# Gated linear attention and a multiplicative FFN: attention products by halves of a chunk's keys, with the masks shared between VectorE and ScalarE

## Chip, cores, metric

One core of a Trainium2 chip. The metric is device time in microseconds (us) from the first to the last instruction, median over several executions; lower is better.

TensorE is PE in the profile (PEld its weight loads), VectorE is DVE, ScalarE is ACT, GpSimd is POOL. L359 is line 359 of that kernel; each kernel has its own line numbers. A matmul in fp32 is two passes, so the counts (x16) of passes are twice the products.

## The reference, cut

```python
# attention: 4 batches, 8 heads, 768 positions, 48 wide
for t in range(S):
    state = alpha[:, :, t, :, None] * state + einsum('bhd,bhe->bhde', k[:, :, t], v[:, :, t])
    y[:, :, t] = einsum('bhd,bhde->bhe', q[:, :, t], state)
# then, on the 3072 x 384 result x (1024 inner):
a, b = x @ w1, x @ w2
out = (a * b @ w3) @ w_out
```

## The kernel before

The sequence is cut into 24 chunks of 128 positions (6 for each batch). In a chunk TensorE makes five groups of products: the old state times q ("state"), the scores k·q, the transposes of the next chunk's q and k, the masked scores times v ("values"), and the outer products for the new state. After the scores VectorE sets the upper triangle of the keys to zero (the mask), and ScalarE copies the transposes out of their banks.

```python
def transposed(n):                       # ... transposes of all heads into two banks tp
    for half in range(2):
        nc.scalar.copy(qkT[:, :, :, ds(DP * half, DP)], tp[half])

def scores(n):
    for j in range(NP):
        for i in range(2):
            r = ds(DP * i, D)
            nc.tensor.matmul(sc[i][:, j, :], qkT[r, 0, j, :], qkT[r, 1, j, :], start=True, stop=True)
    for i in range(2):
        nc.vector.tensor_tensor(ms[:, i].bitcast(I32), sc[i].bitcast(I32), keep_bc, op=ALU.bitwise_and)

def attend(n):
    for j, i, to in heads:
        nc.tensor.matmul(to, vc[:, 2 * j + i, :], ms[:, i, j, :], start=..., stop=...)
    # ... two ScalarE copies of the banks to x, stored to memory
```

The gates x·w1 and x·w2 are exact products of split numbers on the full array. They start as soon as three chunks of x are there, in pieces between the attention's groups; in every fourth chunk (10, 14, 18, 22 counted from 0) there are no pieces left.

```python
for n in range(N + 1):
    # ... loads
    if n: attend_state(n - 1)
    if n < N: scores(n)
    transposed(n + 1)
    if n - 2 in begin: split_x(g, 0)     # ... and new gates queued
    pieces = (0, 3, 3, 2)[(n - 6) % 4] if n > 5 else 0
    # ...
    if n: attend(n - 1)
    outer(n)
    run(pieces > 0)                      # one gate piece: nine passes of 384 columns
    # ... decayed q and k of n + 2, logs, decays; run(pieces > 1), run(pieces > 2)
```

## Time and profile before

| what | value |
|---|---|
| time, median of 3 | 497.57 us (495.11 to 498.14) |
| profiled execution | span 494.5 us, mean granted clock 0.990 |
| first gate product starts | 65.6 us |
| last values product starts | 196.7 us |
| TensorE idle before the first gate / from there to the last values product | 19.2 / 6.5 us |
| from the last values product to TensorE's last pass | 293.9 us, no hole in TensorE (the run ends 3.9 us later) |

The three places in this table cut the run into the *front*, the *middle* (the section in which attention and gates mix) and the *tail*. They come from the starts of single passes in the trace.

### The profile page before, as it was taken

To read this page: it belongs to the slowest core of one execution; us is meant where nothing else is said; L and a number is where in the kernel's file an instruction comes from. 1 tells how busy PE (TensorE), PEld (TensorE's weight loads), DVE (VectorE), ACT (ScalarE), POOL (GpSimd) and SP (SyncE) were. 2 spreads that over 40 slices of the span, in tenths; PEclk is the share of its full clock that TensorE was granted. 3 is DMA by queue.
4 is the path that set the end of the run, shared out by engine and by line. 5 is a ranking of instruction groups with operands and counts; after the bars stand their busy time and mean duration, and the time that the engine had idled before them with its cause. 6 is when DMAs were issued, how large, how long until landed. Compare 5 with 4: busy or idle time off the path is not lost.

```text
span 494.5 us, 9992 instructions
## 1 busy us (share of the span) xinstructions
PE 464.9 (94%) x3808; PEld 423.9 (86%) x3808; DVE 370.0 (75%) x614; ACT 247.8 (50%) x461; POOL 40.0 (8%) x86
## 2 busy tenths in 40 slices
PE   3969779999999999999999999999999999999996
PEld 2747559899898978999999988888888999999996
DVE  2668998998898566999999769686433786667771
ACT  3666758776666553655555444544222533333330
POOL 3123132212102200000000000000000000000000
PEclk9998999999999999999999999999999999999999
DMA  9999999999887933555464433320001875556511
GB/s 174 203 219 199 244 201 229 221 193 254 151 225 144 269 115 113 176 180 198 155 198 156 154 118 117 118 91 34 32 33 56 232 222 178 175 177 175 177 49 48
DMA packets 148032, 79.12 MB, mean 160 GB/s; under 512 B 92176, under 2 KB 141840, under 8 KB 147984
## 3 DMA queue, kind: packets, MB, share of 16 engines
q1 hardware_dynamic: 146704, 78.40, 61.0%
q0 software_dynamic: 1280, 0.08, 0.5%
q8 instruction: 30, 0.49, 0.4%
q14 instruction: 18, 0.15, 0.1%
HBM read 56.40 MB, written 22.06 MB: 159 GB/s over the span
## 4 chain that ended last, share of the span: by engine, by line
PE 78%; DVE 8%; DMA 7%; ACT 3%; issue 2%; SPq 1%; POOL 0%; DVEq 0%; POOLq 0%; ACTq 0%
PE bank L416 40%; PE bank L420 19%; PE bank L465 8%; PE bank L359 2%; PE bank L384 2%; PE bank L282 2%; DMA raw<-in_moe_w_out_dram 2%; PE bank L459 1%; DMA dec<-ends 1%; PE bank L319 1%; DVE ms L362 1%; DVE qk L297 1%; DMA ac<-in_alpha_dram 1%; DMA ends<-e 1%; PE bank L378 1%
## 5 line engine op out<-in xcount | busy, mean ns | idle before, releaser
L416 PE MATMUL bank<-x,w 128*128 128x384 f32 x768 | 160.1, 342 | 0.0
L416 PEld LDWEIGHTS bank<-x,w 128*128 128x128 f32 x768 | 134.2, 188 | 4.8 <-issue 1.9
L418 ACT ACTIVATE t<-bank 128x384 f32<-128x384 f32 x152 | 74.2, 491 | 116.2 <-PE bank L416 101.1
L421 DVE SCALAR_TENSOR_TENSOR r<-bank,t 128x384 f32<-128x384 f32 x128 | 69.1, 552 | 38.5 <-ACT t L418 33.5
L420 PE MATMUL bank<-x,w 128*128 128x384 f32 x384 | 87.9, 336 | 1.5 <-ACT qkT L321 1.2
L420 PEld LDWEIGHTS bank<-x,w 128*128 128x128 f32 x384 | 68.7, 189 | 2.1 <-ACT qkT L321 1.5
L416 PE MATMUL bank<-w3o,ab 128*128 128x384 f32 x384 | 70.4, 334 | 0.0
L416 PEld LDWEIGHTS bank<-w3o,ab 128*128 128x128 f32 x384 | 66.9, 188 | 0.0
L465 PE MATMUL bank<-wo,w3T 128*128 128x384 f32 x128 | 42.6, 486 | 0.0
L200 ACT ACTIVATE rest<-raw 128x512 f32<-128x512 uint32 (+1 forms) x36 | 23.4, 649 | 27.8 <-DMA raw<-in_moe_w_dram 20.9
L420 PE MATMUL bank<-w3o,ab 128*128 128x384 f32 x192 | 37.1, 334 | 0.0
L465 PEld LDWEIGHTS bank<-wo,w3T 128*128 128x128 f32 x128 | 24.2, 189 | 14.9
L484 DVE TENSOR_TENSOR ab<-abl,ab 128x1024 fp32r<-128x1024 f32 x24 | 29.4, 1223 | 9.1 <-ACT ab L483 9.1
L432 DVE TENSOR_TENSOR ab<-r 128x384 f32<-128x384 f32 x64 | 35.5, 554 | 0.9
L483 ACT ACTIVATE ab<-abl 128x1024 fp32r<-128x1024 f32 x24 | 25.5, 1061 | 18.8 <-PE bank L420 18.8
L359 PE MATMUL bank<-qkT 48*128 48x128 f32 x384 | 30.8, 297 | 3.6 <-DVE ms L362 1.8
L321 ACT COPY qkT<-bank 128x512 f32<-128x512 f32 x48 | 25.8, 590 | 16.0 <-PE bank L319 16.0
L420 PEld LDWEIGHTS bank<-w3o,ab 128*128 128x128 f32 x192 | 33.6, 188 | 0.0
L362 DVE TENSOR_TENSOR ms<-bank,keep 128x512 int32<-128x512 int32 x48 | 31.2, 682 | 2.4 <-PE bank L359 2.4
L359 PEld LDWEIGHTS bank<-qkT 48*128 48x128 f32 x384 | 25.9, 198 | 8.2 <-issue 4.2
L205 ACT ACTIVATE power<-power,rebias 128x512 uint32<-128x512 uint32 (+1 forms) x36 | 25.1, 699 | 15.2 <-DVE power L204 15.0
L297 DVE TENSOR_TENSOR qk<-kq,e 128x768 f32<-128x768 f32 x24 | 22.8, 952 | 10.6 <-ACT e L288 9.9
(66 smaller groups left out, 526.7 us busy)
## 6 DMA issues: line engine op xcount, KB each, us to landing
abd<-ab SPq DMA_DIRECT2D x64, 192.0 KB, 2.4
abl<-abd SPq DMA_DIRECT2D x24, 512.0 KB, 4.5
raw<-in_moe_w_dram SPq DMA_DIRECT2D x16, 512.0 KB, 3.8
xT<-xd SPq DMA_DIRECT2D x12, 576.0 KB, 4.3
raw<-in_moe_w_dram SPq DMA_DIRECT2D x24, 256.0 KB, 5.0
kq<-in_k_dram SPq DMA_DIRECT2D x24, 192.0 KB, 5.1
kq<-in_q_dram SPq DMA_DIRECT2D x24, 192.0 KB, 5.1
v<-in_v_dram SPq DMA_DIRECT2D x24, 192.0 KB, 4.6
```

The source lines that it names most:

```text
L297: nc.vector.tensor_mul(qks[n % 3][:, :, :, 0:D], st.pop(("kq", n)), st.pop(("e", n)).rearrange("p i (h d) -> p i h d", h=H))
L321: nc.scalar.copy(qkT[:, :, :, ds(DP * half, DP)], tp[half])
L359: nc.tensor.matmul(sc[i][:, j, :], qkT[r, 0, j, :], qkT[r, 1, j, :], start=True, stop=True)
L362: nc.vector.tensor_tensor(ms[:, i].bitcast(I32), sc[i].bitcast(I32), keep_bc, op=ALU.bitwise_and)
L416: nc.tensor.matmul(p1, w[part][i], x[part][i], start=(part == i == 0), stop=(part == 1 and i == n - 1))
L418: nc.scalar.activation(t, p1, AF.Copy, scale=(1.0 + 1.0 / P) * scale)
L420: nc.tensor.matmul(p2, w[2][i], x[2][i], start=(i == 0), stop=(i == n - 1))
L421: nc.vector.scalar_tensor_tensor(to, p2, -scale, t, op0=ALU.mult, op1=ALU.add)
L432: nc.vector.tensor_mul(ab, *r)
L465: nc.tensor.matmul(po, w3T[:, j, :], wo[:, j, :], start=(j == 0), stop=(j == KF - 1))
L483: nc.scalar.activation(t[:, 0], ab, AF.Copy, scale=1.0 - 2.0 ** -13)
L484: nc.vector.tensor_sub(t[:, 1], ab, t[:, 0].bitcast(FP32))
```

## The change

The intent: in a chunk of 128 positions the keys of the second half never see the queries of the first, so a quarter of scores and values is zero. Cut in halves of the keys, that quarter need not be computed, and only the two diagonal blocks of 64 columns need a mask; the rest is a plain copy, which idle ScalarE can make. Two row halves may not write one bank of the values at once (the rule of banks that the prediction cites), so the values' products now come in two turns. The second turn must not start until the first is surely out; the program ensures it by a dependency on the second copy of the next chunk's transposes, which TensorE makes after the first turn.

```diff
     def transposed(n):
         for half in range(2):
-            nc.scalar.copy(qkT[:, :, :, ds(DP * half, DP)], tp[half])
+            st["copied"] = nc.scalar.copy(qkT[:, :, :, ds(DP * half, DP)], tp[half])
     def scores(n):
         for j in range(NP):
-            for i in range(2):
-                r = ds(DP * i, D)
-                nc.tensor.matmul(sc[i][:, j, :], qkT[r, 0, j, :], qkT[r, 1, j, :], start=True, stop=True)
+            for s in range(2):
+                for i in range(2):
+                    r = ds(DP * i, D)
+                    nc.tensor.matmul(sc[i][hf(s), j, 0:C - DP * s], qkT[r, 0, j, hf(s)], qkT[r, 1, j, DP * s:],
+                                     start=True, stop=True)
         for i in range(2):
-            nc.vector.tensor_tensor(ms[:, i].bitcast(I32), sc[i].bitcast(I32), keep_bc, op=ALU.bitwise_and)
+            nc.vector.tensor_tensor(ms[:, i, :, 0:DP].bitcast(I32), sc[i][:, :, 0:DP].bitcast(I32), keep_bc,
+                                    op=ALU.bitwise_and)
+            nc.scalar.copy(ms[0:DP, i, :, DP:], sc[i][0:DP, :, DP:])
-    def attend(n):
-        for j, i, to in heads:
-            nc.tensor.matmul(to, vc[:, 2 * j + i, :], ms[:, i, j, :], ...)
+    def attend(n, turn):
+        for j in range(HP):
+            for b in range(2):
+                for s in range(2):
+                    jj, i = b * HP + j, turn ^ s
+                    product = tc.keep_in_program_order(nc.tensor.matmul(
+                        to[jj, i][:, DP * s:], vc[hf(s), 2 * jj + i, :], ms[hf(s), i, jj, 0:C - DP * s], ...))
+                    if turn and first:
+                        tc.add_manual_dep(product.ins, st["copied"].ins.name, ...)
 # the loop:
         if n: attend_state(n - 1)
+        if n: attend(n - 1, 0)
         if n < N: scores(n)
         # ...
-        if n: attend(n - 1)
         outer(n)
         run(pieces > 0)
+        if n: attend(n - 1, 1)
```

Cut away: the smaller mask constant, the fixed order of the transposes, and an extra small copy that stands in for "copied" in the last two chunks.

## The prediction

> **What bounds the kernel now.** I read the page first, then the busy time by stretches of 50 us, the chain that ended last, the waits of each engine by stretch, the timeline of TensorE through single chunks, and last the starts of single passes in the trace.
>
> From the page (busy us and share of the span, instructions) and the view of stretches (start and end, length, then busy us of PE, PEld, DVE, ACT, POOL, granted clock, DMA share, GB/s):
>
> ```profile
> PE 464.9 (94%) x3808; PEld 423.9 (86%) x3808; DVE 370.0 (75%) x614; ACT 247.8 (50%) x461; POOL 40.0 (8%) x86
> ...
> 0.00:50.00 50.00, 35.77 (x432) 27.34 (x432) 30.44 (x56) 28.24 (x55) 13.74 (x40) 0.93 1.09 199
> 50.00:100.00 50.00, 42.45 (x578) 36.36 (x579) 46.76 (x80) 35.41 (x70) 11.18 (x16) 0.97 0.99 224
> 100.00:150.00 50.00, 49.30 (x610) 44.88 (x609) 43.30 (x74) 32.83 (x69) 8.43 (x16) 1.00 0.92 206
> 150.00:200.00 50.00, 46.78 (x604) 42.26 (x604) 34.87 (x63) 26.93 (x59) 6.67 (x14) 1.00 0.59 154
> 200.00:250.00 50.00, 50.00 (x290) 50.00 (x290) 49.05 (x94) 28.18 (x52) 0.00 (x0) 1.00 0.58 186
> ```
>
> The attention chunks, which the change touches, fill the first 197 us. To about 65 us TensorE idles often and VectorE's conversions, masks and products are the chain. From the first gate product (65.6 us) TensorE is the bound. From 197 us to the end, nearly 300 us, it runs without a hole, and nothing there is changed. So what counts is TensorE's own time between 65 and 197 us, its holes there, and when the first gate starts.
>
> The groups concerned (busy us, mean ns of one, idle before):
>
> ```profile
> L359 PE MATMUL bank<-qkT 48*128 48x128 f32 x384 | 30.8, 297 | 3.6 <-DVE ms L362 1.8
> L362 DVE TENSOR_TENSOR ms<-bank,keep 128x512 int32<-128x512 int32 x48 | 31.2, 682 | 2.4 <-PE bank L359 2.4
> L321 ACT COPY qkT<-bank 128x512 f32<-128x512 f32 x48 | 25.8, 590 | 16.0 <-PE bank L319 16.0
> ```
>
> A typical chunk in TensorE's timeline (start us, length; state, scores, transposes, values, outer products, then a gate):
>
> ```profile
> 136.04 0.67 PE L378 MATMUL bank<-qkT,T 48*64 48x128 f32 x16
> 136.64 1.16 PE L359 MATMUL bank<-qkT 48*128 48x128 f32 x16
> 137.63 0.66 PE L319 MATMUL bank<-ident,qk 64*128 64x64 f32 x16
> 138.23 1.09 PE L384 MATMUL bank<-ms,v 128*64 128x128 f32 x16
> 139.15 0.62 PE L331 MATMUL bank<-v,qk 128*64 128x48 f32 x16
> 139.70 1.33 PE L416 MATMUL bank<-x,w 128*128 128x384 f32 x6
> ```
>
> The reader is to take the differences of starts, not the lengths: scores 0.99 us, values 0.92, state 0.60, all with sixteen passes (an fp32 product is two). The starts of single passes show why. Scores and values go in pairs on two half arrays, a pair every 112 and 109 ns. The state products, on quarter arrays, go four at a time, also every 109 ns. So a wave of passes with 128 moving columns takes 109 ns whether two or four share it.
>
> **What the Trainium skill says.** "TensorEngine Tiling (Array Packing)", Key Properties: "Changing tiling mode (not just tile) drains the TensorE". The trace agrees: where shape of array changes, the last pass of one group to the first of the next is about 90 ns longer than within a group, and the first wave is longer too. State to scores: 199 and 207 ns against waves of about 110, 0.18 us in all. Transposes to values 153 and 154 against 62 and 109, 0.14 us. Outer products to a gate 152 and 279 against 58 and 173, 0.20 us. Gate to state 268 and 140 against 173 and 109, 0.13 us. "TensorE: Matmul & The Clock Gate", in Part 3 (what overlaps and what doesn't), says matmuls start and end in program order; in this trace a pass never starts before its predecessor. The same page (engine queue depths) says that ScalarE and VectorE are strict first in, first out; the trace orders them so, and I build on it below. "PSUM — Partial Sum Buffer", on bank collisions: two engines may not use the same bank and quadrant at once, and different row tiles may not write one bank at once. The kernel before has no pair that shows it; the changed program obeys it, with ScalarE's copy of a score bank waiting for VectorE's mask of it, and the values' products split in two turns.
>
> **The change part by part.**
>
> Scores. Eight products on half arrays become sixteen on quarters, 128 and 64 columns alternating. The triangle saves a quarter of the columns, but a wave of four lasts as long as its 128-column members, since the next wave's first product needs the same quarter. 32 passes in waves of four are 8 waves x 109 = 0.87 us, as against 8 x 112 = 0.90. Values: 32 passes, 8 waves x 109 = 0.87 us, exactly as now. So TensorE gains 0.03 us a chunk, about 0.5 us over the 16 chunks after the first gate.
>
> Switches of the array's shape. Now a chunk is gate, quarters (state), rows (scores, transposes), columns (values, outer), gate. After: gate, quarters (state, first turn of values, scores), rows (transposes), columns (outer), gate, quarters (second turn), gate. I counted them in the two programs' order from the first gate to the last values' product: 74 now, 97 after. 13 second turns stand between two gates. Into gates +13 at 0.20 = +2.6 us; into scores -16 at 0.18 = -2.9; into transposes +15 at about 0.16 (my estimate between the cases above) = +2.4; into outer products +13 at 0.14 = +1.8; two fewer others, -0.3. Sum +3.6 us; with the 0.5 gained, TensorE's own work grows by 3.1 us.
>
> Masks. VectorE takes 682 ns for 512 columns, and other reads of a bank 552 for 384 and 351 for 192, about 0.15 us plus 1.04 ns a column. 256 columns are 0.42 us. 48 of them: 12.6 us of VectorE's 370 go. In the chain before the first gate, from 35 to 65 us, there are the masks of some five chunks, ten x 0.26 = 2.6 us. TensorE, ScalarE and a busy DMA share that stretch, so I count 1.5 us.
>
> ScalarE. 48 copies of 256 columns at 394 ns (the row of the copies to x) are 18.9 us more. It was busy 60 to 70% between 60 and 150 us, so it doesn't become the bound, but its order matters, next.
>
> New waits. The first product of the second turn waits for the second copy of the next chunk's transposes, which stands in ScalarE's order behind the two score copies, which wait for the masks. Counted from the end of the scores: mask lag L, two masks 0.75, a score copy 0.4, two transposed copies 1.1, together L + 2.25 us. TensorE comes there after transposes, outer products and one gate piece, at about +3.0. So it stands when L exceeds some 0.6 us. In the trace before L was, for chunks 8 to 23 (counted from 0), 0.0, 1.0, 2.3, 0.7, 1.4, 0.2, 2.3, 1.9, 0.0, 0.8, 2.1, 1.3, 0.0, 2.0, 3.0, 0.0. In the chunks with gates I let the lighter VectorE take 0.4 us from each: 12, 15, 19 and 21 stand by about 0.4, 0.9, 0.3 and 0.9, together 2.5 us. In the four chunks without gates (10, 14, 18, 22) TensorE has nothing to fill with: state, second turn, first turn and scores now wait for masks, two score copies and the transposed copies in a row. Now the next scores start at +3.2 us and the values take 0.9 later; after, the second turn can start at about +3.7 and the scores at +4.7: 0.6 us each, 2.4 in all.
>
> Sum: -1.5 + 3.1 + 2.5 + 2.4 = +6.5 us on 497.6, thus 504.
>
> **The rivals.** First: VectorE's relief carries through. It is busy 47 of 50 us between 50 and 100 us, and three of the largest holes of TensorE there are its own:
>
> ```profile
> PE bank L319 <- DVE qk L297: 2.3, 1, 2.3
> PE bank L282 <- ACT la L266: 1.7, 1, 1.7
> PE bank L359 <- DVE ms L362: 0.6, 1, 0.6
> ```
>
> All holes between the first gate and 197 us make 6.4 us. Had the change removed them all, with 2.6 from the front and no new wait, 9.0 less 3.1 would leave -6 us: 491.5. Against it: the mask is replaced by a longer chain over two engines, so the holes with "DVE ms" hardly go.
>
> Second: ScalarE's strict order makes the new waits worse than I count. A score copy that waits for a mask also holds up the copies that free a gate's bank, and then gate products stand. With L not lowered at all, L - 0.6 sums to 4.7 us over the gate chunks; if each of the 12 loses another 0.4 to such holes and the short ones 1.5 each, that is 15.5 us of waits in place of 4.9: 515.
>
> Third: issue. 64 passes now follow one another at 27 ns each, where only 16 did. If the sequencer can't feed them, say 35 ns, each chunk loses 0.5 us, 8 us over 16 chunks: 512. The state products' 27 ns speak against it, though their queue had been filled during a gate.
>
> **Range and chances.** The first rival in full gives 491, the second or third in full 512 to 515; halves of them bound my range at 496 and 513. A gain over 2% (under 487.6) has no source: 4%. A loss over 2% (above 507.5) needs a good half of the second or third rival: 26%. Within 2%: 70%.
>
> **What would show each step.** Single passes of scores and values in waves of four at 109 ns: then no gain in TensorE's own time. If the 64-column members let the next wave in early (waves near 80 ns), scores and values together gain 0.4 us a chunk and the prediction is 6 us too high. Second turns followed by a gate whose first pass comes after 200 ns and first wave takes 280: the switches. Mask near 0.42 us, score copy near 0.39. In the waits, second turn on the transposed copies near 5 us in all; far more means the second rival, near zero makes the time 499 or less. First gate at 63 to 65 us. After the last values' product, the same 297 us to the end; if that differs, my picture is wrong.

## More of the kernel before

The prediction shows the page's totals, stretches, groups and chain; one row of the page that it does not show matters later, the granted TensorE clock in 40 equal slices, in tenths of full speed:

```profile
PEclk9998999999999999999999999999999999999999
```

Here 9 is 90% or more. Only one slice near 40 us is lower.

## The result

| | before | after |
|---|---|---|
| median, range, 4 runs each | 496.34 us (494.94 to 498.14) | 525.31 us (521.33 to 526.06) |
| ratio | | 1.0571 (1.0510 to 1.0631) |
| profiled span, mean clock | 494.5 us, 0.990 | 519.6 us, 0.962 |
| first gate product | 65.6 us | 68.9 us |
| last values product | 196.7 us | 223.4 us |
| TensorE idle, front / middle | 19.2 / 6.5 us | 20.0 / 14.4 us |
| tail | 293.9 us | 292.3 us |

A ratio here and below is the mean time of one kernel's runs over that of the other's of the same rounds, with a 95% interval, so not quite the ratio of the medians. Executions over 1.5% slower than the fastest of the same kernel are left out of the means.

The change costs nearly 29 us, far outside the predicted range. The profiled pair differs by 25.1 us, and all of that lies before the last values product. The page after, its totals and clock row, and the stretches of 50 us (start and end, length, busy us of PE, PEld, DVE, ACT, POOL, clock, DMA share, GB/s):

```profile
PE 481.4 (93%) x4576; PEld 430.7 (83%) x4576; DVE 361.4 (70%) x615; ACT 264.4 (51%) x517; POOL 37.0 (7%) x86
...
PEclk9978899989899699899999999999999999999999
```

```profile
100.00:150.00 50.00, 46.86 (x729) 40.03 (x729) 33.19 (x61) 32.60 (x73) 7.77 (x16) 0.90 0.81 179
150.00:200.00 50.00, 43.16 (x649) 37.27 (x647) 28.41 (x54) 25.83 (x61) 6.38 (x13) 0.90 0.62 150
```

Two things differ from before. Between 100 and 200 us, the two stretches shown, TensorE is idle more (3.1 and 6.8 us of each 50, before 0.7 and 3.2). And the clock, which was 1.00 in those stretches, is 0.90. Note also that TensorE's busy time rose by 16.5 us although its predicted extra work was 3: an instruction at a lower clock is busy for longer.

TensorE's waits after (engine, line waited for: us in all, times, longest):

```profile
PE bank L408 <- ACT qkT L325: 11.8, 11, 4.3
PE bank L389 <- ACT ms L373: 6.4, 4, 2.1
PE bank L454 <- ACT ms L373: 1.6, 2, 0.9
```

L408 is the values' product, L325 the copy of the transposes, L389 the state product, L373 the new score copy. None of these three rows has a counterpart of any size before.

One hole shows how they arise. The kernel before, iteration without gate pieces, VectorE and TensorE (start us, length; in brackets the idle time before and what ended it):

```profile
124.32 1.36 DVE L407 SCALAR_TENSOR_TENSOR x<-x,xT 128x1152 fp32r<-128x1152 f32 x1
125.59 1.29 DVE L362 TENSOR_TENSOR ms<-bank,keep 128x512 int32<-128x512 int32 x2
```

```profile
123.14 0.66 PE L319 MATMUL bank<-ident,qk 64*128 64x64 f32 x16
123.73 1.09 PE L384 MATMUL bank<-ms,v 128*64 128x128 f32 x16
124.66 0.62 PE L331 MATMUL bank<-v,qk 128*64 128x48 f32 x16
125.21 0.44 PE L378 MATMUL bank<-qkT,T 48*64 48x128 f32 x4
126.34 0.65 PE L378 MATMUL bank<-qkT,T 48*64 48x128 f32 x12 [0.69 <-DVE ms L362]
```

The same iteration after, for VectorE, ScalarE and TensorE:

```profile
132.99 0.95 DVE L300 TENSOR_TENSOR qk<-kq,e 128x768 f32<-128x768 f32 x1
133.86 0.95 DVE L271 TENSOR_TENSOR la<-la,la 128x768 fp32r<-128x768 f32 x1
134.72 0.75 DVE L371 TENSOR_TENSOR ms<-bank,keep 128x256 int32<-128x256 int32 x2
```

```profile
135.18 0.36 ACT L373 COPY ms<-bank 64x256 f32<-64x256 f32 x1 [2.52 <-DVE ms L371]
...
136.19 0.59 ACT L325 COPY qkT<-bank 128x512 f32<-128x512 f32 x1
```

```profile
131.92 0.71 PE L323 MATMUL bank<-ident,qk 64*128 64x64 f32 x16
132.56 0.67 PE L335 MATMUL bank<-v,qk 128*64 128x48 f32 x16
133.16 0.43 PE L389 MATMUL bank<-qkT,T 48*64 48x128 f32 x4
135.59 0.74 PE L389 MATMUL bank<-qkT,T 48*64 48x128 f32 x10 [2.00 <-ACT ms L373]
136.83 1.34 PE L408 MATMUL bank<-ms,v 64*64 64x128 f32 x25 [0.27 <-ACT qkT L325]
```

Count from the end of the scores (the start of the transposes) to the state product that goes on. Before it is 126.34 - 123.14 = 3.20 us, of which the values' product fills 0.93. After it is 135.59 - 131.92 = 3.67 us, and the values fill nothing of it: their first turn went ahead of the scores, and their second turn is what waits last. So the change took a filler out of the hole and put a copy at its end; the hole grew from 0.69 to 2.00 us. In the chunk at 170 us the waits come to 5.4 us, 4.32 of them at the second turn.

And then the clock falls. Pieces of a gate in the trace of the kernel after, one at 104.48 after the hole of 100 us, one at 116.22:

```profile
104.48 2.29 PE L450 MATMUL bank<-x,w 128*128 128x384 f32 x6
106.57 1.16 PE L454 MATMUL bank<-x,w 128*128 128x384 f32 x3
...
116.22 1.33 PE L450 MATMUL bank<-x,w 128*128 128x384 f32 x6
117.40 0.69 PE L454 MATMUL bank<-x,w 128*128 128x384 f32 x3
```

From start to start the six passes take 2.09 us in the one and 1.18 in the other. The trace lists the granted clock in time: it is half speed from 101.7 to 108.5. The other stretches at half speed of this execution (leaving out one at its very end) are 33.4 to 40.2, 50.5 to 53.9, 64.1 to 67.5, 135.8 to 139.2, 173.4 to 183.6 and 210.9 to 214.3; before there were two, 34.6 to 41.5 and 72.2 to 75.6. Every start lies on one grid of 3.413 us. Counting TensorE's idle time in each square of the grid, the squares that ended in a drop had 3.06, 2.52, 3.32, 1.77, 2.00, 2.74 and 1.62 us; squares at full speed with 1.21 or less did not (in the trace before, 1.50 did not and 1.65 did).

"TensorE: Matmul & The Clock Gate", Part 1 (the HAM clock gate), in the Trainium skill states this mechanism: a free-running window of 3413 ns, and half the clock for an array that was idle. The trace agrees on the grid, and its clock record shows full and half and nothing between; steady gate passes come every 320 ns instead of 173, 1.85 times as long. The prediction had cited other parts of that page and left this one out.

Split of the 25.1 us of the profiled pair. "Half clock" is half of TensorE's busy time in the stretches at half speed (a little too much where gates run, since 147 of 320 ns are 46%); "rest" is what is left. Nine gate passes moved from the tail into the middle (324 against 315), 1.56 us, taken off the one and added to the other:

| part | longer by | idle | half clock | rest |
|---|---|---|---|---|
| front | 3.4 | 0.7 | (12.1 - 6.6) / 2 = 2.75 | -0.1 |
| middle, without the nine passes | 21.8 | 8.0 | (21.6 - 3.4) / 2 = 9.1 | 4.7 |
| tail, with the nine passes | 0.0 | 0 | 0 | 0 |

The front's share is the least sure. Five of the kernels traced (before, and four of the experiments below) have the same front, and their first gate came anywhere from 63.4 to 67.7 us.

### The profile page after: what moved, and what is told of

The parts are those of the page before. It is cut to its first block, busy times and chain, and to the rows that moved or that the text cites.

```text
span 519.6 us, 11585 instructions
## 1 busy us (share of the span) xinstructions
PE 481.4 (93%) x4576; PEld 430.7 (83%) x4576; DVE 361.4 (70%) x615; ACT 264.4 (51%) x517; POOL 37.0 (7%) x86
## 4 chain that ended last, share of the span: by engine, by line
PE 72%; DVE 6%; DMA 4%; ACT 3%; issue 2%; SPq 1%; DVEq 0%; ACTq 0%
PE bank L450 37%; PE bank L454 18%; PE bank L499 8%; PE bank L408 3%; PE bank L367 2%; PE bank L493 1%; ACT qkT L325 1%; PE bank L323 1%; DMA raw<-in_moe_w_dram 1%; DMA raw<-in_moe_w_out_dram 1%; ACT ms L373 1%; DMA xd<-x 1%; DMA kq<-in_q_dram 1%; PE bank L335 1%; DVE x L441 1%
## 5 line engine op out<-in xcount | busy, mean ns | idle before, releaser
L450 PE MATMUL bank<-x,w 128*128 128x384 f32 x768 | 163.0, 347 | 0.0
L454 PE MATMUL bank<-x,w 128*128 128x384 f32 x384 | 88.3, 337 | 1.6 <-ACT ms L373 1.6
L454 PEld LDWEIGHTS bank<-x,w 128*128 128x128 f32 x384 | 69.2, 190 | 2.3 <-ACT ms L373 2.3
L408 PE MATMUL bank<-ms,v 64*64 64x128 f32 (+1 forms) x768 | 35.5, 283 | 11.8 <-ACT qkT L325 11.8
L408 PEld LDWEIGHTS bank<-ms,v 64*64 64x64 f32 x768 | 26.1, 154 | 19.3 <-ACT qkT L325 17.1
L367 PE MATMUL bank<-qkT 48*64 48x128 f32 (+1 forms) x768 | 37.1, 291 | 0.0
L454 PE MATMUL bank<-w3o,ab 128*128 128x384 f32 x192 | 37.1, 334 | 0.0
L499 PEld LDWEIGHTS bank<-wo,w3T 128*128 128x128 f32 x128 | 24.2, 189 | 14.9
L454 PEld LDWEIGHTS bank<-w3o,ab 128*128 128x128 f32 x192 | 33.6, 188 | 0.0
L373 ACT COPY ms<-bank 64x256 f32<-64x256 f32 x48 | 16.6, 365 | 30.9 <-DVE ms L371 30.9
L367 PEld LDWEIGHTS bank<-qkT 48*64 48x64 f32 x768 | 30.8, 157 | 1.1 <-issue 1.1
```

What stands on the lines that cost most here:

```text
L367: nc.tensor.matmul(sc[i][hf(s), j, 0:C - DP * s], qkT[r, 0, j, hf(s)], qkT[r, 1, j, DP * s:], start=True, stop=True)
L408: product = tc.keep_in_program_order(nc.tensor.matmul(to[jj, i][:, DP * s:], vc[hf(s), 2 * jj + i, :], ms[hf(s), i, jj, 0:C - DP * s], sta ...
L450: nc.tensor.matmul(p1, w[part][i], x[part][i], start=(part == i == 0), stop=(part == 1 and i == n - 1))
L454: nc.tensor.matmul(p2, w[2][i], x[2][i], start=(i == 0), stop=(i == n - 1))
L499: nc.tensor.matmul(po, w3T[:, j, :], wo[:, j, :], start=(j == 0), stop=(j == KF - 1))
```

## The experiments

The theories. **W1**: the second turn waits for the transposed copies, which stand on ScalarE behind score copies that wait for VectorE's masks; take one link out and most of the loss goes. **K**: the holes also halve TensorE's clock for a while, so they cost more than their length. Its rival **N**: holes cost their length and no more, and the rest is TensorE's own additional work. Each kernel ran in several rounds with the kernel before on the same chip; the medians of the kernel before were 496.65, 497.01 and 497.52 us in the three groups. All the kernels gave right results.

Two columns need a word. Each execution's record has its span and mean clock, and the clock is either full or half, so span x (1 - clock) is half of the time at half speed: what the low clock costs if TensorE is busy throughout. It is an upper figure, as some of that time is idle. It is a mean over all fast runs; "idle" is TensorE's in the middle of the one profiled run.

| kernel | median us (range) | ratio (95%) | mean span | clock loss | span less loss | idle, middle |
|---|---|---|---|---|---|---|
| before (23 runs) | 497.01 | | 495.2 | 7.2 | 488.0 | 6.5 |
| after (5 runs; the median is of four) | 525.31 | 1.0571 | 523.0 | 24.1 | 499.0 | 14.4 |
| scores by quarters | 496.80 (496.23-498.36) | 1.0026 (0.9973-1.0078) | 495.3 | 8.2 | 487.1 | 5.1 |
| rest by VectorE | 515.00 (511.26-516.97) | 1.0379 (1.0311-1.0446) | 512.8 | 15.8 | 497.0 | 13.6 |
| copies first | 511.43 (510.14-515.11) | 1.0332 (1.0256-1.0409) | 510.3 | 19.7 | 490.6 | 8.6 |
| seen | 514.82 (514.21-515.91) | 1.0387 (1.0334-1.0439) | 513.2 | 20.8 | 492.4 | 10.0 |
| values' turns alone | 511.88 (511.01-513.69) | 1.0313 (1.0282-1.0344) | 510.4 | 15.8 | 494.6 | 7.8 |
| filler | 526.25 (521.14-528.43) | 1.0583 (1.0522-1.0644) | 523.8 | 10.8 | 513.0 | 14.0 |
| before, one piece kept (19 runs; one slow run of 502.86 us left out) | 497.04 (494.00-499.66) | 1.0006 (0.9988-1.0024) | 495.6 | 7.6 | 488.0 | 4.9 |
| copies first, one piece kept | 504.30 (502.44-506.26) | 1.0156 (1.0120-1.0192) | 502.6 | 13.3 | 489.3 | 6.5 |

So over all runs the change costs 523.0 - 495.2 = 27.8 us, of which 24.1 - 7.2 = 16.9 are clock by this upper figure. The profiled run was the fastest; by the same figure it has some 14.5, by the busy time in the split above 11.9.

### Scores by quarters, in the kernel before

```diff
-            for i in range(2):
-                nc.tensor.matmul(sc[i][:, j, :], qkT[r, 0, j, :], qkT[r, 1, j, :], start=True, stop=True)
+            for s in range(2):
+                for i in range(2):
+                    nc.tensor.matmul(sc[i][ds(DP * s, DP), j, :], qkT[r, 0, j, ds(DP * s, DP)], qkT[r, 1, j, :],
+                                     start=True, stop=True)
```

> The kernel before with one part of the change alone: scores as sixteen products on quarter arrays (the second half of the keys over all 128 columns, so that every element is written), masks on 512 columns by VectorE and values as before. Theory W (the loss comes from the second turn of the values and from the score copies on ScalarE, as waits of TensorE with a halved clock after them): the quarters cost nothing, 494 to 499 us, ratio 0.995 to 1.005. Rival Q (quarter products are slower for TensorE, in issue or in switches): 500 us or more. Waves of four at 109 ns in the trace are what both should show if W is right.

496.80 us, the same as before. Twice as many products on quarters of the array, at 128 columns each, cost nothing: TensorE's idle time in the middle is no longer (5.1 us), though it lies elsewhere (3.5 us of waits for the mask at the state product, before 0.7), and the clock loss is near that of before. The scores' new form isn't the cause. Issue (the third rival of the prediction) isn't either: in the kernel after, the 64 passes of a chunk from state to scores take 1.89 us (188.91 to 190.80), 30 ns each with the drains of the switches in it, where the rival needed 35 without them.

### The rest of the scores copied by VectorE

```diff
-            nc.scalar.copy(ms[0:DP, i, :, DP:], sc[i][0:DP, :, DP:])
+            nc.vector.tensor_copy(out=ms[0:DP, i, :, DP:], in_=sc[i][0:DP, :, DP:])
```

> The changed kernel with the rest of the scores copied by VectorE in place of ScalarE; TensorE's order is all but the same. Theory W1 (the second turn waits for the transposed copies, which ScalarE holds back behind score copies that wait for masks): the wait of the second turn for the transposed copies falls from 11.8 us to under 4, fewer stretches of half clock, 503 to 512 us, although VectorE has 48 operations of some 0.4 us more. Rival Q2 (the two turns with their switches of the array's shape cost it, whoever copies): 518 us or more. Rival V (VectorE's lag is what counts): the lag grows, the first products of the next chunk wait for VectorE, 520 us or more.

515.00 us, some 10 less than after. TensorE's waits of this run:

```profile
PE bank L408 <- ACT qkT L325: 9.4, 5, 3.2
PE bank L389 <- DVE ms L373: 4.0, 4, 1.2
PE bank L454 <- DVE ms L373: 3.7, 4, 1.6
```

The second turn now stands 5 times rather than 11, but waits for VectorE take the place of those for ScalarE: a gate piece (L454) and the state product (L389) need banks that VectorE frees later. The idle time of the middle hardly falls (13.6 us). W1's forecast (this wait under 4 us, 503 to 512 us) was missed on both counts, and its rivals' (518 us or more) too. The link over ScalarE is a part of the loss, and moving it isn't a cure.

### Copies of the transposes first on ScalarE

Only ScalarE's order changes: the masks and score copies of a chunk are put behind its transposed copies.

```diff
+            st["copied"] = tc.keep_in_program_order(nc.scalar.copy(qkT[...], tp[half]))
     def scores(n):
+        st["sc", n] = sc
+    def masks(n):                        # the mask and copy loop, moved here
+            tc.keep_in_program_order(nc.scalar.copy(ms[0:DP, i, :, DP:], sc[i][0:DP, :, DP:]))
 # the loop:
         transposed(n + 1)
+        if n < N: masks(n)
```

> The changed kernel with ScalarE's order alone changed: the two transposed copies stand before the two score copies of a chunk. Theory W1: the second turn's wait for the transposed copies falls from 11.8 us to under 4; the state products' wait for a bank that a score copy frees (6.4 us) stays or grows, since that copy now comes later; 506 to 516 us. Rival Q2: 518 us or more.

511.43 us, 14 less than after with the same instructions. Of TensorE's waits for these copies the largest is the second turn's (L412):

```profile
PE bank L412 <- ACT qkT L325: 7.5, 4, 3.2
```

The waits of the state product and the gate for the score copy (6.4 and 1.6 us after) are gone, with 0.5 and 2.0 us for the transposed copies in their place, and of the second turn's eleven waits four are left. The middle's idle time is 8.6 us, and "span less loss" is 490.6, only 2.6 above before. The time lies where W1 had it (506 to 516 us), but the wait was to fall under 4 us and is 7.5, and the state product's wait was to stay. So W1 holds in part: its link is worth half of the loss, and no run that took out one link gave back more. Of the 15.1 us that are left against before, 12.5 are clock (19.7 against 7.2). In this run, too, the front alone had 24.2 us of busy time at half speed, although its idle time (15.3 us) was the shortest of all. How often the clock falls is not read from the sum of the holes alone.

### The second turn waits for the first by a small copy

```diff
+        if turn == 0:
+            for i in range(2):
+                for b in range(2):
+                    st["seen", n] = nc.scalar.copy(seen[hf(b), i:i + 1], to[b * HP + HP - 1, i][:, C - 1:])
-                        tc.add_manual_dep(product.ins, st["copied"].ins.name, ...
+                        tc.add_manual_dep(product.ins, st["seen", n].ins.name, ...
```

> The changed kernel with the second turn waiting not for the transposed copies but for four tiny copies by ScalarE that read the first turn's banks, issued right after the first turn; the score copies stay where they are. Theory W1: the second turn hardly waits (under 3 us), but ScalarE has 96 tiny copies (some 0.2 us each, 19 us) more and the waits for score copies stay: 508 to 518 us. Rival Q2: 520 us or more.

514.82 us, 10.5 less than after, 3.4 more than with the order changed. The second turn's waits on transposed copies vanish (it still waits 4.1 us, for score copies and for the small ones), but the scores wait for those copies instead (3.7 us, 5 times), and the state product still waits for score copies (4.3 us, 4 times). A wait moved is not a wait removed; cutting the dependency helped as far as it shortened holes (10.0 us idle).

### The values' turns alone

Scores and masks are as before, only the values come in two turns:

```diff
-                        to[jj, i][:, DP * s:], vc[hf(s), 2 * jj + i, :], ms[hf(s), i, jj, 0:C - DP * s],
+                        to[jj, i][:, DP * s:], vc[hf(s), 2 * jj + i, :], ms[hf(s), i, jj, DP * s:],
 # scores(n): products on half arrays and one mask of 512 columns by VectorE, as before
```

> The values' two turns alone: scores as full products and masks on 512 columns by VectorE, both as before; the second turn still waits for the transposed copies, but no score copy stands before them on ScalarE. If the two turns (their switches, and a wait in the middle of a chunk) are what is left of the loss once the score copies are out of the way, this lies where the two mended versions lie, 508 to 515 us, and TensorE's section from the first gate to the last values has 4 to 5 us that are neither holes nor half clock. Rival: quarter scores or the score copies carry the rest of the loss, then 497 to 504 us.

511.88 us: a half of the whole loss is in the two turns, without any score copy. Against before, the middle of its profiled run is longer by 12.6 us without the nine passes: 1.3 idle, 5.8 half clock, 5.5 rest. The rest is the same size in all kernels with two turns (3.9 to 5.5 us; the filler's kernel, with its own passes, aside) and absent with the scores' quarters (-0.3): so it is most likely the cost of the turns' own passes and switches. This is by difference; no run isolates a single switch.

### A filler where TensorE has no gate

```diff
+    def filler(k):
+        d = bank()[:, 0:C]
+        for _ in range(k):
+            tc.keep_in_program_order(nc.tensor.matmul(d, ident, ident, start=True, stop=True))
         outer(n)
+        if n > 1 and not pieces and n < N:
+            filler(8)
```

> The changed kernel with eight useless 128-column fp32 products (some 1.7 us of TensorE) after the outer products of each chunk that has no gate, where the holes are; they feed nothing. Theory K (the halved clock after a hole costs as such): the stretches of half clock go from 24 us in the section to under 10, and the kernel gets faster although work is added: 510 to 519 us. Rival N (the clock only accompanies the holes; the holes are the loss): no faster, 524 to 535 us, since the products take up the holes or lengthen the chunks.

526.25 us, no better than after. Taken by what was expected, this is N's forecast (524 to 535 us) and not K's (510 to 519, under 10 us of half clock in the middle; there were 17.1). But it doesn't decide. The clock loss did fall from 24.1 to 10.8 us, as K would have it. But the scheduler moved the second turn ahead of the state product, so that it waited longer than ever for the transposed copies: 17.7 us, 12 times. With the fillers' own time (nine chunks of 16 passes at 109 ns, some 7 us in the middle and 9 before the first gate) that took back all of it. A cleaner test of K was needed, away from the attention.

### One gate piece kept for the chunks without gates, before and with copies first

```diff
         transposed(n + 1)
+        if n - 2 in begin and n > 6:
+            run(1)
+            pieces = 0
...
-        pieces = (0, 3, 3, 2)[(n - 6) % 4] if n > 5 else 0
+        pieces = (0, 3, 3, 1)[(n - 6) % 4] if n > 6 else 0
```

The same lines go into the kernel before and into "copies first".

> The kernel before with one gate piece held back from each group for the chunk without gates (pieces 0,3,3,2 become 1 held back,3,3,1). A possible better version: the holes of 0.6 to 1.2 us in those chunks (some 4 of 6.5 us) are filled with useful work; but the split of the next group waits for the piece. 490 to 496 us if the filling works, 497 to 503 if the later split costs as much.

> The version with the transposed copies first, and one gate piece held back for each chunk without gates. Theories W1 and K: its remaining holes (8.6 us in the section, nearly all in the chunks without gates) and half-clock stretches (11.9 us) shrink: 499 to 507 us. If the two turns cost more than the holes and the clock, it stays at 509 to 514.

In the kernel before it is worth nothing (497.04, ratio 1.0006): its holes there are short. With copies first it is 504.30 us, 7 less than without: the useful work fills the holes (idle 6.5 us in the middle, as before), and the clock loss falls from 19.7 to 13.3. That is the best form of the change that was found, and still 1.6% (1.2 to 1.9%) slower than the kernel before, clear of noise though under 2%: 4 us of rest in the middle stay, and nothing in the change pays for them. No version beat the kernel before.

### Holes in the tail of the kernel before

K and N are tested where nothing else happens: in the gates after the attention, where TensorE has no hole at all. ScalarE makes one, three or five idle copies (616 ns each) after a gate piece, and the next piece waits for the last of them. Eight places were meant; only seven came about, as the traces have 7, 21 and 35 of these copies.

```diff
+    def hole():
+        for i in range(copies):          # 1, 3 or 5
+            c = tc.keep_in_program_order(nc.scalar.copy(pz, w12[:, 0, 0, 0, 0:CW].bitcast(FP32)))
+            if i == 0: after_(c, st["product"])     # starts when the piece before has ended
+        st["hold"] = c                              # the next piece's first product waits for it
 # the loop over the gates:
+        if i in range(4, 48, 6):
+            hole()
```

> The kernel before, with eight artificial holes in its unbroken stretch of gates (after 197 us, where TensorE alone sets the time and nothing of the change is at work): before each of eight gates, TensorE waits for one ScalarE copy of 0.5 us that itself waits for the product before. Holes of some 0.8 us, 6 us in all. Theory K (a hole costs its length, and a long one also a stretch of half clock): too short for the clock, so the time grows by about the holes, +5 to +8 us, 502 to 506. Theory N: the same.

> The same eight places with three copies each, holes of some 1.7 us, 14 us in all. Theory K: where most of the hole lies within one 3.4 us window of the clock, half clock follows for one window or more, 1.7 us each; perhaps half of them do, so +18 to +28 us, 515 to 525, with three to eight stretches of half clock in the trace. Theory N: +12 to +15 us, 509 to 512.

> The same eight places with five copies each, holes of some 2.6 us, 21 us in all. Theory K: nearly every hole brings one or two windows of half clock, +32 to +50 us, 529 to 547, in the trace some eight stretches of half clock between 200 and 400 us, gates that take twice as long in them. Theory N: +19 to +23 us, 516 to 520.

The rest of the tail is as before, with the same number of gate passes. TensorE's wait for the copies in the run with five (us in all, times, longest; with one and three copies it is 6.9 and 16.1 us, 7 times each):

```profile
PE bank L428 <- ACT pz L417: 26.7, 7, 5.1
```

| copies | median us, ratio (95%) | tail longer by | holes | at half clock, busy; half of it | rest |
|---|---|---|---|---|---|
| 1 | 506.13, 1.0165 (1.0110-1.0221) | 302.8 - 293.9 = 8.9 | 6.9 | 0; 0 | 2.0 |
| 3 | 520.50, 1.0431 (1.0362-1.0500) | 316.4 - 293.9 = 22.5 | 16.1 | 9.9; 4.9 | 1.5 |
| 5 | 538.96, 1.0848 (1.0779-1.0917) | 335.6 - 293.9 = 41.7 | 26.7 | 28.3; 14.2 | 0.8 |

(One of the four runs with three copies took 1166.58 us at full clock; it is left out. Nothing here explains it.)

The holes were longer than their copies, as other ScalarE work came between; so the sums that were expected are compared by the holes as they were. N fails: with five copies the holes explain 26.7 of 41.7 us, and the half clock's 14.2 nearly all of the rest. With 46% for the half (the 147 of 320 ns above) what remains is 2.0, 1.9 and 2.0 us, the same for the seven restarts in each kernel. The gate pieces after a hole with three copies show it (start to start of six passes 1.15 us, then 1.91; the length, 2.12 us, is 1.24 again in the next piece):

```profile
236.28 1.31 PE L428 MATMUL bank<-x,w 128*128 128x384 f32 x6 [2.01 <-ACT pz L417]
237.43 0.96 PE L435 MATMUL bank<-x,w 128*128 128x384 f32 x3
238.19 2.12 PE L428 MATMUL bank<-x,w 128*128 128x384 f32 x6
240.10 1.13 PE L435 MATMUL bank<-x,w 128*128 128x384 f32 x3
241.06 1.24 PE L428 MATMUL bank<-x,w 128*128 128x384 f32 x6
```

Here the drop does not come in the hole but 1.4 us after its end, at the edge of the grid (237.66 us). Which of the seven holes with three copies drop the clock is decided by how they lie on the grid:

| hole, us | parts in two squares | clock after |
|---|---|---|
| 2.67 | 1.18 + 1.49 | full |
| 2.01 | 2.01 + 0 | half, 3.4 us |
| 2.01 | 1.26 + 0.75 | full |
| 2.01 | 0.73 + 1.28 | full |
| 2.60 | 0.08 + 2.52 | half, 3.4 us |
| 2.38 | 0.60 + 1.78 | full |
| 2.38 | 2.01 + 0.37 | half, 3.4 us |

No hole with one copy (0.71 to 1.55 us) dropped it, and all seven with five (3.31 to 5.08 us) did, two of them for 6.8 us. So a hole has two prices: its length, always, and some 1.7 us (half of 3.4) if two microseconds or so of it fall into one square. Equal holes of 2.01 us cost 2 or nearly 4 us by luck; this fits the spread between runs of one kernel, e.g. the clock loss of the kernel after from 19.7 to 26.2 us, though no run tests that.

## Why the prediction was wrong

It said 504 us (496 to 513); measured were 525.31. Its sum, term by term, against the profiled pair (25.1 us):

| the prediction's term | predicted | measured |
|---|---|---|
| lighter masks, front | -1.5 | +0.6 without the clock |
| TensorE's own work | +3.1 | +4.7 |
| second turns, chunks with gates | +2.5 | 0.0 (3.2 against 3.1 idle) |
| four chunks without gates | +2.4 | +7.9 (11.25 against 3.32 idle) |
| clock, front and middle | not thought of | +2.75 + 9.1 |
| sum | +6.5 | +25.1 |

**The step that failed** is the sum itself, in which "New waits" went in at their length. A hole was taken to cost what it lasts; the tail's holes show that it can cost nearly twice as much, and the clock is the largest term: 11.9 us in the profiled pair, and up to 16.9 as a mean over the runs. The signs were on the page before: a slice of 0.8 in the clock row, and 0.93 and 0.97 in the stretches that the prediction quotes, just where TensorE had holes.

**The second failure** is the size of one term. "In the four chunks without gates ... 0.6 us each" was 0.6 to 4.6 us each (idle of 1.8, 2.3, 5.4 and 1.8 us, before 0.6, 0.7, 0.8 and 1.2). The mechanism was named rightly (masks, two score copies and transposed copies in a row, with nothing to fill), and so was its formula: the second turn came 4.1, 4.9, 7.1 and 4.1 us after the scores' end, and L + 2.25 with the lags L of this trace (1.9, 2.8, 5.0 and 2.0) gives as much, to 0.2 us. The slip is "about +3.7": with the prediction's own lags (2.3, 2.3, 2.1, 3.0, less 0.4 for the relief) its formula gives 4.0 to 4.9, some 2.3 us more in all. The rest of the miss is one chunk, where L was 5.0. There ScalarE and VectorE had both stood idle (3.0 and 2.4 us, until 165.88) for a load of weights that they convert, so the split of x behind these conversions came late: VectorE's part, two operations of 1.35 us and ahead of the mask, began only at 169.68. Whether the change delayed that load isn't shown. In the chunk shown above, the decayed product and the log split stood ahead of the mask (134.72 us), where before there was only the split. For the chunks with gates the opposite error was made; the gate piece covers the wait there. So the total of the second turn's waits, predicted near 5 us, was 11.8 (7.4 of it in the middle), with 6.4 more at the state product (4.3 in the middle).

**TensorE's own work** was right in its kind and near in size: +4.7 by difference for the predicted +3.1, and the experiments put it on the values' turns. The gaps at the switches were as predicted (from a gate to the second turn 268 ns and then 93; from the second turn to a gate 199 and 279). But "a pass never starts before its predecessor" does not hold for quarters. In the trace after:

```profile
95.21 0.50 PE L408 MATMUL bank<-ms,v 64*64 64x128 f32 x14
95.45 0.30 PE L367 MATMUL bank<-qkT 48*64 48x128 f32 x2
95.54 0.28 PE L408 MATMUL bank<-ms,v 64*64 64x128 f32 x2
```

The source fixes the order of the values' products, 128 and 64 columns in turn, with 64 columns last. Yet the last four passes to start are all of 128 columns (95.43 to 95.55), the last one of 64 columns started at 95.41, and two score passes come between. (The order of the compiled program is not in the trace; that it keeps the fixed order is assumed.) The passes of 64 columns run ahead; those with 128 columns set the end, as they would in waves of four, so no time came of it.

**VectorE's relief** was real (416 ns a mask rather than 682, predicted 420; the score copy 365 ns, predicted 390) and of no use: the first gate came at 68.9 us, not at 63 to 65, as front holes halved the clock there as well (12.1 us of busy time, before 6.6; by how much the change did that is unsure, as said above).

**The tail** stayed as predicted: 292.3 us against 293.9, the difference being the nine gate passes that had moved forward.

**The rivals.** The first (relief carries through) is refuted. The second (ScalarE's order) was the right direction: undoing the order gives back 14 us, more than its own calculation had. The third (issue) is refuted by the scores' quarters and by the 1.89 us for 64 passes. (The range, too, was not what its rule gives: halves of the rivals would be 498 and 508 to 510, not 496 and 513.)

Open: why two squares without any idle time (from 101.7 and 176.8 us in the kernel after), filled with small attention passes, did not lift the clock, while others did; and whether one could keep both the change's order and the clock with a filler that the scheduler leaves in place.

## What to carry to other kernels

When a change can open holes in TensorE, count each hole twice: once by its length, and once for the clock if some two microseconds of it can fall into one window of 3.4 us; the clock row of the page tells where this already happens. Before splitting a product in two turns, ask what it had been filling: here the values' product was the work that covered the wait for the masks. And a dependency that hangs on a convenient later instruction takes over everything that stands ahead of that instruction on its engine.

## What the Trainium skill lacked or had wrong

- "TensorE: Matmul & The Clock Gate", Part 1 gives half the clock "after ≥1 idle window (~3.4µs)", and its section "Why this matters for your kernels" asks for "No PE-idle gaps >~3µs between matmul bursts". Here much less was enough: holes of 2.01 us with 2.01 us in one window (the tail, three copies), and 1.62 us of idle time in one window in the kernel after; 1.78 us in another case did not suffice. Gaps of 2 us are not safe. The free-running window of 3413 ns agrees, and so does the clock of a half, though gate passes took 320 ns instead of 173.
- The same page has the clock rise after one busy window. Windows filled all but wholly with small passes on quarters and halves of the array (32 score passes and 16 transposes in each) can fail to lift it: after the drops at 101.7 and 173.4 us it stayed low for 6.8 and 10.2 us, though the windows from 101.7 and from 176.8 us had no idle time.
- The same page, Part 3, says that matmuls start in strict program order. On different quarters of the array they seem not to: the last values' pass of 64 columns started at 95.41 us, before four of 128 columns (95.43 to 95.55) that precede it in the order that the source fixes.
- "TensorEngine Tiling (Array Packing)", Key Properties, says that a change of mode drains, without a figure. In the trace before, the first pass after a switch came some 90 ns later than passes within a group, and the next wave 31 to 106 ns late (gate to state 268 and 140 ns against 173 and 109; outer products to a gate 152 and 279 against 58 and 173).
